# Attention with bilinear experts: three units of folded weights behind one product, the fourth ahead of the next read

## The chip, the cores and the metric

The kernel runs on one core of a Trainium2 chip. The metric is the device time of that core for one launch, in microseconds (us), lower is better. The engines are named as the profile names them: PE is TensorE, with PEld its weight loads, DVE is VectorE, ACT is ScalarE, SP is the queue that issues most DMAs.

## The reference

```python
scores = x @ state.T / sqrt(D);  a = softmax(scores);   xread = a @ state      # B=8, H=8, S=512, Ns=32, D=64
scores2 = state @ x.T / sqrt(D); a2 = softmax(scores2); sread = a2 @ x
rows = concat([xread, sread], axis=2)   # per batch 512 + 32 rows of 512
out = (((rows @ w1) * (rows @ w2)) @ w3) @ w_out                               # 512 -> 1024 -> 1024 -> 512
```

Everything is float32, and there is no nonlinearity behind the product of `rows @ w1` and `rows @ w2`.

## The kernel before

**Algebra.** `w3 @ w_out` is multiplied out once (`wo`). For the 512 x rows of a batch the read `a @ state` is not made: the state is multiplied into the weights instead. Such a product of one half of the hidden columns and of `w1` or `w2` is a **unit** (`unit` in `sw_steps`, L275 to L280): 16 matmuls by `per_head` (L148) into a two-bank PSUM tile, then `split` (L95): ACT casts it to a high part (`sw_hi`, L98) and DVE subtracts that from the tile to get the low part (`sw_lo`, L99). A batch needs four units; the first two serve its hidden tiles 0 to 3, the last two its tiles 4 to 7. Large products are made of such pairs, as high x high + high x low + low x high.

**Batches.** Batch 0 and the weights' preparation come first. Batches 1 to 7 run in `quarter_batch` (L513), one after the other, and at the end `state_rows` makes the rows of `sread`. One batch has two stages:

- Stage one is a loop over eight hidden tiles. A tile is 12 matmuls on L318 (6 for `w1`, 6 for `w2`), which fill a two-bank PSUM tile `ps`. ACT copies one bank out (`tmp`, L521), DVE multiplies it with the other (`hidden_quarters`, L401), and then the PSUM tile is free. Behind tile 1 stand three more things in PE's order: the batch's state read (L250, 64 matmuls, `reads[b]`), then the scores of the next batch (L148, 16 matmuls with `x_d`).
- Stage two (`stage2_quarters`, L453) multiplies the eight tiles by `wo` in seven products of halves: four on L432/L437, three on L444/L449. Behind the first product stand two units of the next batch, behind the second the other two.

**The softmaxes** (`scores`, L180) work on the scores of the next batch in one two-bank PSUM tile. DVE takes the maxima of the state softmax (L194), transposes the tile for the x softmax (L191) and scales the maxima (L195); ACT then makes the two exponentials of the state softmax (L204, each followed by the read of its accumulator). These are the last readers of that PSUM tile. L211 to L228 are the x softmax on DVE and ACT, whose result `at` is the moving operand of the next batch's stage one. `scores` is a generator: it goes on by one `yield` behind tile 2, one behind tile 4 and to its end behind the second product. At its end 16 DMAs move blocks of the exponentials (`e<-work`, L172), for the next state read.

**Order.** PE and SP issue in the order in which the code is written. ACT and DVE are ordered by a list scheduler when the program is built, within `high_priority` and `issue_after` constraints; on the chip each engine works its list in order.

**PSUM.** `two_banks` (L92) hands out three buffers in turn. Tiles, scores, units and the three products on L444 all take from it, so a tile waits for the release of whatever stands three requests before it. Before the change the requests behind tile 1 are: scores, tile 2, tile 3, tile 4. Tile 4 thus takes the scores' buffer.

Of the kernel before, what the change touches and what calls it, by code (L numbers as in the profile page):

```python
# [27 lines left out]
ALU = mybir.AluOpType  # L28
# [8 lines left out]
PLAIN = 1  # L37

@with_exitstack
def attn_bilinear_kernel(  # L40
# [10 lines left out]
    nc = tc.nc  # L51
# [124 lines left out]
    def attention_steps(b):  # L176
        xd = x_tiles[b]
        a2 = {}

        def scores():  # L180

            ps = two_banks()
            per_head(ps, b, lambda rows, j: xd[rows, j])
            yield
            flat = lambda t: t.rearrange("p k s -> p (k s)")

            s1 = work_tile()
            m2 = att.tile([P, KT], F32, name="m2")

            def turn():  # L190
                nc.vector.transpose(out=flat(s1), in_=flat(ps))  # L191

            def maxima():
                nc.vector.tensor_reduce(out=m2, in_=ps, axis=AX.X, op=ALU.max)  # L194
                nc.vector.tensor_scalar_mul(m2, m2, -SCALE)  # L195

            for step in (maxima, turn) if b > PLAIN else (turn, maxima):
                step()
            e2 = att.tile([P, KT, S], F32, name="e2", bufs=1)
            sum2 = att.tile([P, KT], F32, name="sum2")  # L200
            a2["e"], a2["sum"] = e2, sum2
            for kt in range(KT):
                one = slice(kt, kt + 1)
                nc.scalar.activation(  # L204
                    out=e2[:, kt], in_=ps[:, kt], func=AF.Exp, bias=m2[:, one], scale=SCALE, accum_out=sum2[:, one]
                )

            J = KT * S // NS
            s1v = flat(s1).rearrange("p (j n) -> p j n", n=NS)
            m1 = att.tile([P, J], F32, name="m1")  # L210
            nc.vector.tensor_reduce(out=m1, in_=s1v, axis=AX.X, op=ALU.max)  # L211
            nc.vector.tensor_tensor(
                out=s1v, in0=s1v, in1=m1.unsqueeze(2).broadcast_to([P, J, NS]), op=ALU.subtract
            )
            nc.scalar.activation(out=s1, in_=s1, func=AF.Exp, scale=SCALE)
            yield
            nc.vector.tensor_scalar_add(sum2, sum2, 1e-9)
            nc.vector.reciprocal(out=sum2, in_=sum2)
            sum1 = att.tile([P, J], F32, name="sum1")
            nc.vector.tensor_reduce(out=sum1, in_=s1v, axis=AX.X, op=ALU.add)  # L220
            nc.vector.tensor_scalar_add(sum1, sum1, 1e-9)
            nc.vector.reciprocal(out=sum1, in_=sum1)
            nc.vector.tensor_tensor(
                out=s1v, in0=s1v, in1=sum1.unsqueeze(2).broadcast_to([P, J, NS]), op=ALU.mult
            )
            yield
            at = work_tile()
            nc.vector.transpose(out=flat(at), in_=flat(s1))  # L228
            at_tiles[b] = [att.tile([P, KT, S], F32R, name=f"at_{part}", bufs=1) for part in ("hi", "lo")]
            last = split(*at_tiles[b], at)  # L230
            yield

            blocks = work_tile()
            with tc.issue_after(last[1].ins):
                nc.vector.transpose(out=flat(blocks), in_=flat(e2))
            a2["t"] = work_tile() if b < PLAIN else att.tile([P, KT, S], F32, name="e2", bufs=1)
            tiles = lambda t: t.rearrange("p k (t m) -> p (k t) m", m=P)
            move_blocks(lambda its, j: tiles(a2["t"])[its, :, j * NS:(j + 1) * NS],
                        lambda mine, c: tiles(blocks)[mine, :, c * NS:(c + 1) * NS])

        def read_state():

            xs = token_tiles[b]

            ps = (bank() if b else two_banks()[:, 0])[:, :KT * D].rearrange("p (k d) -> p k d", k=KT)
            for kt in range(KT):
                for t in range(NT):
                    for j in range(NP):
                        mine = slice(j * NS, (j + 1) * NS)
                        nc.tensor.matmul(  # L250
                            ps[mine, kt], a2["t"][:, kt, t * P + j * NS:t * P + (j + 1) * NS],
                            xs[:, t, 2 * j + kt], start=(t == 0), stop=(t == NT - 1),
                        )
            scaled = att.tile([P, KT, D], F32, name="scaled", bufs=1)
            a2["read"] = nc.vector.tensor_tensor(
                out=scaled, in0=ps, in1=a2["sum"].unsqueeze(2).broadcast_to([P, KT, D]), op=ALU.mult
            )
            turned = att.tile([P, KT, D], F32, name="turned")
            nc.vector.transpose(
                out=turned.rearrange("p k d -> p (k d)"), in_=scaled.rearrange("p k d -> p (k d)")  # L260
            )
            yield
            move_blocks(lambda its, j: sread[its, j, b * NS:(b + 1) * NS],
                        lambda mine, c: turned.rearrange("p k (c n) -> p (k c) n", n=NS)[mine, c])

        return scores, read_state, a2


# [3 lines left out]
    def sw_steps(b):  # L272
        sw_tiles.setdefault(b, {})

        def unit(half, i):  # L275
            ps = two_banks()
            as_q = ps.rearrange("p k (c f) -> p k c f", c=2)
            per_head(as_q, b, lambda rows, j: w_sb[rows, 2 * half:2 * half + 2, i, j])
            sw_tiles[b][half, i] = sw_pair()
            split(*sw_tiles[b][half, i], ps)  # L280

        return [(lambda half=half, i=i: unit(half, i)) for half in range(HALF) for i in range(2)]
# [66 lines left out]
    reads = {}  # L349
# [41 lines left out]
    def hidden_quarters(a, b, ft, q):  # L391

        p, kk = divmod(ft, 2)
        first, second = slice(0, HT), slice(HT, S)
        if ft == QF:
            q["late"] = late.tile([P, QF, S], F32, name="raw")
        elif ft < QF and kk == 0:
            q["raw"].append(main.tile([P, 2, NF], F32, name="g_x", bufs=2))
        whole = q["raw"][p][:, kk] if ft < QF else q["late"][:, ft - QF]
        with tc.high_priority():  # L400
            nc.vector.tensor_tensor(out=whole, in0=a, in1=b, op=ALU.mult)  # L401
        if ft == 0:
            q["a11"], q["s3"] = quarter_pairs(), quarter_pairs()
        elif ft == QF:
            q["a12"] = quarter_pairs()
        if not kk:
            return
        raw = q["raw"][p % 2]
        if ft < QF:
            split(*q["a11"][p], raw[:, :, first])  # L410
            s3 = by_two(tmp_tile())
            nc.vector.tensor_tensor(out=s3, in0=raw[:, :, first], in1=raw[:, :, second], op=ALU.subtract)
            split(*q["s3"][p], s3)
        else:
            i = p - 2
            half = q["late"][:, 2 * i:2 * i + 2]
            split(*q["a12"][i], half[:, :, first])
            nc.vector.tensor_tensor(out=raw[:, :, second], in0=raw[:, :, second], in1=half[:, :, second], op=ALU.add)
            nc.vector.tensor_tensor(out=raw[:, :, first], in0=raw[:, :, second], in1=raw[:, :, first], op=ALU.subtract)
            nc.vector.tensor_tensor(out=half[:, :, first], in0=half[:, :, first], in1=raw[:, :, first], op=ALU.subtract)  # L420
# [32 lines left out]
    def stage2_quarters(b, q, units, more):  # L453
# [56 lines left out]
        sum3(m1, bank_f)  # L510
        stored_quarter(m1, 0, 1)

    def quarter_batch(b):  # L513
        q = {"raw": []}
        w = sw_steps(b + 1) if b + 1 < B else [lambda: None] * 4
        softmax = iter(())
        for ft in range(FT):
            ps = stage1_sums(b, ft)
            a_sb = tmp_tile()
            with tc.high_priority():  # L520
                nc.scalar.copy(out=a_sb, in_=ps[:, 0])  # L521
            hidden_quarters(a_sb, ps[:, 1], ft, q)
            if ft == 1:
                run([reads[b]])
                if b + 1 < B:
                    scores, reads[b + 1], _ = attention_steps(b + 1)
                    softmax = scores()
                    next(softmax)
                    load_tokens(b + 1)
                if b + 2 < B:  # L530
                    load_x(b + 2)
            elif ft in (2, 4):
                next(softmax, None)
            if b == PLAIN and ft == 1:
                combine_weights(QF - 1)
        stage2_quarters(b, q, w[:2], [*w[2:], lambda: softmax])

    def run(steps):
        for step in steps:
# [204 lines left out]
```

## Time and profile before

| | |
|---|---|
| median of 3 runs | 491.81 us (491.71 to 491.94) |
| the profiled execution's own time | 491.68 us |
| its span | 489.9 us |
| PE busy | 483.7 us (99%), granted clock 1.0 |
| DVE busy | 390.3 us (80%) |
| ACT busy | 238.6 us (49%) |

The span is what the profile covers; the remaining 1.8 us lie around it. A busy PE is not a PE at its peak, since matmuls are pipelined and their ends are modelled: where PE waits is seen better in the start times of its instructions. Batch 1 lies at about 119.6 to 168.4 us of the span, batch 4 at 264.9 to 313.1 us, and `state_rows` begins at about 452 us.

### The profile page before, as it was taken

What the parts mean: (1) busy time and instruction counts of PE and PEld (TensorE: products, weight loads), DVE (VectorE), ACT (ScalarE), POOL (GpSimd) and SP (SyncE); (2) the same over time, 40 slices, a digit from 0 to 9 for tenths busy, and PEclk for the clock granted to TensorE, in tenths of its full rate; (3) what the DMA queues carried; (4) which work ended last, traced back from release to release, by engine and by line L of the source; (5) the groups of instructions that cost most, each with busy time, mean ns of one, the idle gap of its engine ahead of it and who ended that gap; (6) DMA issues with size and microseconds to landing.
All of it is one profiled execution on the core that took longest, in us unless ns stands there. A gap on an engine that the chain in (4) does not pass through costs nothing.

```text
span 489.9 us, 8603 instructions
## 1 busy us (share of the span) xinstructions
PE 483.7 (99%) x3390; PEld 369.0 (75%) x3390; DVE 390.3 (80%) x576; ACT 238.6 (49%) x364; POOL 0.2 (0%) x4
## 2 busy tenths in 40 slices
PE   8999999999999999999999999999999999999996
PEld 6444467767787878787888778877887788899885
DVE  5669897699899779958995899599859985578870
ACT  4767794454357045704570556055505650354640
POOL 0000000000000000000000000000000000000000
PEclk9999999999999999999999999999999999999999
DMA  8995971153113404130423042204220222001101
GB/s 341 391 405 177 371 300 27 17 216 64 36 24 160 110 25 179 35 97 4 180 45 86 5 180 50 80 5 179 48 82 6 89 52 78 7 2 43 45 2 43
DMA packets 56361, 52.49 MB, mean 107 GB/s; under 512 B 42752, under 2 KB 50944, under 8 KB 51712
## 3 DMA queue, kind: packets, MB, share of 16 engines
q1 hardware_dynamic: 47488, 43.27, 26.7%
q10 hardware_dynamic: 8832, 8.65, 5.1%
q8 instruction: 27, 0.44, 0.4%
q14 instruction: 14, 0.11, 0.1%
HBM read 38.27 MB, written 8.91 MB: 96 GB/s over the span
## 4 chain that ended last, share of the span: by engine, by line
PE 92%; DVE 3%; ACT 2%; DMA 1%; issue 0%; ACTq 0%; DVEq 0%
PE ps L318 34%; PE ps_o L432 11%; PE ps L444 8%; PE ps L148 7%; PE ps_o L332 7%; PE ps_o L437 5%; PE ps L449 4%; PE ps L682 3%; PE ps_o L575 3%; PE ps_o L562 3%; PE ps L562 3%; PE ps L684 2%; PE ps_o L250 1%; DMA raw<-in_w_k_dram 1%; DVE m L194 0%; ACT ulps L127 0%
## 5 line engine op out<-in xcount | busy, mean ns | idle before, releaser
L318 PE MATMUL ps<-at_lo,sw_hi 128*128 128x512 f32 x256 | 101.8, 398 | 0.2 <-ACT e L204 0.2
L318 PE MATMUL ps<-at_hi,sw_hi 128*128 128x512 f32 x256 | 99.8, 390 | 0.0
L318 PE MATMUL ps<-at_hi,sw_lo 128*128 128x512 f32 x256 | 99.6, 389 | 0.0
L521 ACT COPY tmp<-ps 128x512 f32<-128x512 f32 x56 | 32.8, 586 | 125.1 <-PE ps L318 114.3
L318 PEld LDWEIGHTS ps<-at_lo,sw_hi 128*128 128x128 f32 x256 | 48.1, 188 | 17.8 <-DVE g_x L401 5.4
L318 PEld LDWEIGHTS ps<-at_hi,sw_lo 128*128 128x128 f32 x256 | 48.1, 188 | 10.3
L318 PEld LDWEIGHTS ps<-at_hi,sw_hi 128*128 128x128 f32 x256 | 48.1, 188 | 9.5 <-issue 0.2
L460 DVE TENSOR_TENSOR tmp<-tmp,ps 128x512 f32<-128x512 f32 x42 | 28.9, 687 | 16.9 <-PE ps L449 15.9
L401 DVE TENSOR_TENSOR g_x<-tmp,ps 128x512 f32<-128x512 f32 x28 | 19.1, 682 | 28.7 <-ACT tmp L521 28.7
L99 DVE TENSOR_TENSOR sw_lo<-ps,sw_hi 128x1024 fp32r<-128x1024 f32 (+1 forms) x34 | 38.2, 1145 | 0.2 <-ACT sw_hi L98 0.2
L98 ACT CAST g_hi<-raw 128x512 fp32r<-128x512 f32 x42 | 24.1, 618 | 23.7 <-DVE raw L401 14.5
L98 ACT CAST sw_hi<-ps 128x1024 fp32r<-128x1024 f32 (+1 forms) x34 | 31.1, 966 | 2.8 <-PE ps L148 2.7
L432 PEld LDWEIGHTS ps_o<-wo,g_hi 128*128 128x128 f32 x224 | 28.2, 191 | 5.6 <-issue 5.0
L99 DVE TENSOR_TENSOR g_lo<-raw,g_hi 128x512 fp32r<-128x512 f32 x42 | 28.0, 681 | 5.2 <-PE ps_o L437 2.8
L432 PEld LDWEIGHTS ps_o<-t,g_hi 128*128 128x128 f32 x224 | 27.8, 192 | 5.0 <-issue 5.0
L98 ACT CAST g_hi<-g_x 128x512 fp32r<-128x512 f32 x42 | 26.0, 622 | 11.4 <-DVE g_x L401 6.0
L148 PE MATMUL ps<-w_sb,st 64*32 64x512 f32 (+1 forms) x544 | 31.4, 570 | 0.0
L432 PE MATMUL ps_o<-t,g_hi 128*128 128x256 f32 x224 | 29.8, 286 | 0.0
L432 PE MATMUL ps_o<-wo,g_hi 128*128 128x256 f32 x224 | 29.7, 286 | 0.0
L99 DVE TENSOR_TENSOR g_lo<-g_x,g_hi 128x512 fp32r<-128x512 f32 x42 | 27.4, 678 | 1.8 <-PE ps_o L437 1.8
L575 PE MATMUL ps_o<-w_sb,w 128*128 128x512 f32 x64 | 28.5, 599 | 0.0
L444 PE MATMUL ps<-t,g_hi 128*128 128x512 f32 x112 | 28.0, 392 | 0.0
(103 smaller groups left out, 785.0 us busy)
## 6 DMA issues: line engine op xcount, KB each, us to landing
raw<-in_w_k_dram SPq DMA_DIRECT2D x8, 1024.0 KB, 6.3
x_d<-in_x_d_dram SPq DMA_DIRECT2D x8, 1024.0 KB, 6.6
raw<-in_w_dram SPq DMA_DIRECT2D x8, 1024.0 KB, 6.3
x_s<-in_x_s_dram SPq DMA_DIRECT2D x8, 1024.0 KB, 5.0
out_dram<-tmp ACTq DMA_DIRECT2D x56, 128.0 KB, 1.8
raw<-in_w3t_dram SPq DMA_DIRECT2D x4, 1024.0 KB, 5.9
e<-work SPq DMA_DIRECT2D x112, 32.0 KB, 2.0
sread<-turned SPq DMA_DIRECT2D x128, 4.0 KB, 1.7
```

The costliest lines, as they stand in the source:

```text
L98: nc.scalar.copy(out=hi, in_=src),
L99: nc.vector.tensor_tensor(out=lo, in0=src, in1=hi.bitcast(F32), op=ALU.subtract),
L148: nc.tensor.matmul(ps[j * NS:(j + 1) * NS, q], sts[b][rows, j], moving(rows, j), start=True, stop=True)
L318: nc.tensor.matmul(ps[:, i], w[:, kt, c:c + P], a[:, kt], start=(k == 0), stop=(k == 3 * KT - 1))
L332: nc.tensor.matmul(ps[:, :DO], g, wo[w][:, ft, :], start=(ft == 0 and k == 0), stop=(ft == FT - 1 and k == 2))
L432: nc.tensor.matmul(ps[:, tt * HO:(tt + 1) * HO], g, w(part, k), start=(fresh and k == 0 and tt == 0 and part == "lo"), stop=False, skip_gr ...
L437: nc.tensor.matmul(ps[:, tt * HO:(tt + 1) * HO], g, w("hi", k), start=False, stop=(k == QF - 1), skip_group_check=True)
L444: nc.tensor.matmul(ps[:, tt].rearrange("p (n d) -> p n d", n=2), g, w(k), start=(k == 0), stop=False, skip_group_check=True,)
L460: sum2 = lambda out, x, y: nc.vector.tensor_tensor(out=out, in0=x, in1=y, op=ALU.add)
L521: nc.scalar.copy(out=a_sb, in_=ps[:, 0])
L562: nc.tensor.matmul(w34_ps[i][:, :DO], chunks[k][:, DO + i * P:DO + (i + 1) * P], w_out[k], start=(k == 0), stop=(k == FT - 1),)
L575: nc.tensor.matmul(w34_ps[i][:, :DO], w3s[i][:, k * P:(k + 1) * P], w_out[k], start=(k == 0), stop=(k == FT - 1))
```

## The change

Four edits, which belong together:

1. `stage2_quarters` gets three units (`units[:3]`) behind the first product of halves and none behind the second, where only the rest of the softmax stands.
2. The fourth unit is kept in `late_units` and runs in the next batch behind tile 1, ahead of the state read and of the scores. In batch 1 that list is empty.
3. For the scores made in these batches, `scores` has one more `yield`, between the exponentials of the state softmax and the x softmax.
4. Behind tile 2 the generator goes on twice; the second piece, the start of the x softmax (L211), is held back until tile 2's product on DVE (L401) has been issued.

```diff
                 nc.scalar.activation(
                     out=e2[:, kt], in_=ps[:, kt], func=AF.Exp, bias=m2[:, one], scale=SCALE, accum_out=sum2[:, one]
                 )
+            if b > PLAIN:
+                yield
...
         with tc.high_priority():
-            nc.vector.tensor_tensor(out=whole, in0=a, in1=b, op=ALU.mult)
+            q["whole"] = nc.vector.tensor_tensor(out=whole, in0=a, in1=b, op=ALU.mult)
...
+    late_units = []
+
     def quarter_batch(b):
         q = {"raw": []}
-        w = sw_steps(b + 1) if b + 1 < B else [lambda: None] * 4
...
             if ft == 1:
-                run([reads[b]])
+                run([*late_units, reads[b]])
...
-            elif ft in (2, 4):
+            elif ft == 2:
+                next(softmax, None)
+                with tc.issue_after(q["whole"].ins):
+                    next(softmax, None)
+            elif ft == 4:
                 next(softmax, None)
...
-        stage2_quarters(b, q, w[:2], [*w[2:], lambda: softmax])
+        units = sw_steps(b + 1) if b + 1 < B else []
+        late_units[:] = units[3:]
+        stage2_quarters(b, q, units[:3], [lambda: softmax])
```

How the instructions stand now is shown at three places of batch 4. Lines of the changed kernel are two or three higher from L211 on (L211 became L213, L401 L403, L432 L434, L521 L524); a number behind a name tells one buffer from another.

PE, behind the first product of halves (`wo,g_hi` and `wo,g_lo`); `w_sb,st` is a unit, `t` stands for the combined weights of the second product. Before:

```order
L437 MATMUL ps_o<-wo,g_lo 128x256 x8
L148 MATMUL ps_2852<-w_sb,st 32x512 x8
L148 MATMUL ps_2865<-w_sb,st 32x512 x8
L432 MATMUL ps_o<-t,g_hi 128x256 x16
L437 MATMUL ps_o<-t,g_lo 128x256 x8
L148 MATMUL ps_2912<-w_sb,st 32x512 x8
L148 MATMUL ps_2925<-w_sb,st 32x512 x8
L432 MATMUL ps_o<-wo,g_hi 128x256 x16
```

Now, the same place:

```order
L439 MATMUL ps_o<-wo,g_lo 128x256 x8
L148 MATMUL ps_2852<-w_sb,st 32x512 x8
L148 MATMUL ps_2865<-w_sb,st 32x512 x8
L148 MATMUL ps_2878<-w_sb,st 32x512 x8
L434 MATMUL ps_o<-t,g_hi 128x256 x16
L439 MATMUL ps_o<-t,g_lo 128x256 x8
L434 MATMUL ps_o<-wo,g_hi 128x256 x16
```

The third product now follows the second directly. The unit that is missing here stands in the next batch between the last matmul of tile 1 and the state read.

DVE, from tile 1's product to tile 2's (`g_x<-tmp,ps_2684`); `g_lo` are low parts of tiles 0 and 1, `scaled` and `turned` belong to the state read, `m_2702` are the maxima of the state softmax and `ps_2669` the scores. Before:

```order
L401 TENSOR_TENSOR g_x<-tmp,ps_2594 128x512
L412 TENSOR_TENSOR tmp<-g_x 128x512
L255 TENSOR_TENSOR scaled<-ps_o,sum_2173 128x128
L99 TENSOR_TENSOR g_lo<-g_x,g_hi 128x512
L99 TENSOR_TENSOR g_lo<-tmp,g_hi 128x512
L259 STREAM_TRANSPOSE turned<-scaled 128x128
L194 TENSOR_REDUCE m_2702<-ps_2669 128x2
L191 STREAM_TRANSPOSE work<-ps_2669 128x1024
L195 TENSOR_SCALAR m_2702<-m_2702 128x2
L211 TENSOR_REDUCE m_2710<-work 128x32
L401 TENSOR_TENSOR g_x<-tmp,ps_2684 128x512
```

Now:

```order
L403 TENSOR_TENSOR g_x<-tmp,ps_2581 128x512
L414 TENSOR_TENSOR tmp<-g_x 128x512
L99 TENSOR_TENSOR g_lo<-g_x,g_hi 128x512
L99 TENSOR_TENSOR sw_lo<-ps_2603,sw_hi 128x1024
L99 TENSOR_TENSOR g_lo<-tmp,g_hi 128x512
L257 TENSOR_TENSOR scaled<-ps_o,sum_2173 128x128
L261 STREAM_TRANSPOSE turned<-scaled 128x128
L194 TENSOR_REDUCE m_2702<-ps_2669 128x2
L191 STREAM_TRANSPOSE work<-ps_2669 128x1024
L195 TENSOR_SCALAR m_2702<-m_2702 128x2
L403 TENSOR_TENSOR g_x<-tmp,ps_2684 128x512
L213 TENSOR_REDUCE m_2710<-work 128x32
```

The low part of the fourth unit (`sw_lo`) now stands ahead of the scores' maxima, and the x softmax begins behind tile 2's product instead of ahead of it.

ACT, from the copy of tile 1 to the exponentials (`e_2706`) and the copies of tile 2 (`ps_2684`) and tile 3 (`ps_2714`). Before:

```order
L521 COPY tmp<-ps_2594 128x512
L98 CAST g_hi<-g_x 128x512
L98 CAST g_hi<-tmp 128x512
L521 COPY tmp<-ps_2684 128x512
L204 ACTIVATE e_2706,sum_2707<-ps_2669,m_2702 128x512 x2
L521 COPY tmp<-ps_2714 128x512
```

Now:

```order
L524 COPY tmp<-ps_2581 128x512
L98 CAST g_hi<-g_x 128x512
L98 CAST sw_hi<-ps_2603 128x1024
L98 CAST g_hi<-tmp 128x512
L204 ACTIVATE e_2706,sum_2707<-ps_2669,m_2702 128x512
L524 COPY tmp<-ps_2684 128x512
L204 ACTIVATE e_2706,sum_2707<-ps_2669,m_2702 128x512
L524 COPY tmp<-ps_2714 128x512
```

The unit's cast is new here, and the copy of tile 2 moved from ahead of both exponentials to between them. Batches 2, 3, 5 and 6 read the same at these two places. In batch 1, which has no late unit, this stretch of both engines is as before; batch 7 has the late unit and no scores.

## Prediction

> **What bounds the kernel now.** I read the page first, then the chain of work that ended last, then the timeline of each engine in one batch.
>
> ```profile
> PE 483.7 (99%) x3390; PEld 369.0 (75%) x3390; DVE 390.3 (80%) x576; ACT 238.6 (49%) x364; POOL 0.2 (0%) x4
> ```
>
> The chain in the window of batch 4 (start, length, what) consists of PE alone:
>
> ```profile
> 265.05 5.46 PE ps L318 x24
> 270.52 1.03 PE ps_o L250 x64
> 271.55 1.02 PE ps L148 x16
> 272.57 16.66 PE ps L318 x72
> ...
> 292.10 1.88 PE ps L148 x32
> 293.98 2.11 PE ps_o L432 x16
> ...
> 298.92 2.11 PE ps_o L432 x16
> ...
> 302.00 1.92 PE ps_o L432 x16
> ...
> 313.26 0.93 PE ps L318 x4
> ```
>
> A batch takes 313.26 - 265.05 = 48.21 us, and PE works through it without a visible hole. So an edit counts only if it shortens PE's own list or makes PE wait. Waits of 0.1 us show in the start times. Here PE goes from tile 3 to tile 4 of batch 4, and then PEld at the same place:
>
> ```profile
> 277.84 0.39 PE L318 MATMUL ps<-at_hi,sw_lo 128*128 128x512 f32 x1
> 278.07 0.49 PE L318 MATMUL ps<-at_lo,sw_hi 128*128 128x512 f32 x1
> 278.39 0.40 PE L318 MATMUL ps<-at_hi,sw_hi 128*128 128x512 f32 x1
> ...
> 278.05 0.19 PEld L318 LDWEIGHTS ps<-at_lo,sw_hi 128*128 128x128 f32 x1 [0.25 <-ACT e L204]
> ```
>
> Tile 4's first weights waited 0.25 us for the exponentials, which read the scores out of the buffer that tile 4 takes. PE lost 0.1 us by it (0.32 us from start to start, where its neighbour has 0.23). This handover is already just in time: whatever comes later there, PE waits for in full.
>
> **The change part by part.** The frame is batch 4; batches 2 to 6 have the same new order.
>
> *Fewer turns on PE.* The product on L432 takes 2.11 us behind units and 1.92 us behind another product, 0.19 us less. Before, two products of a batch stand behind units, now one. The units themselves stay four a batch, at 1.88 / 2 = 0.94 us each. No row shows a unit between tile 1 and the state read: the nearest is the x16 group of the scores, 1.02 us, against 0.94 in a pair. So the move costs between 0 and 0.08 us; it could be below nothing only if the read behind it got shorter, for which I see no reason. I take 0, since the place already changes from L318 to small matmuls once. Six batches (1 to 6) save 6 x 0.19 = 1.14 us.
>
> *The late unit on DVE and ACT.* Here are the two engines' lists as they ran before; for the unit's price, a pair of casts and one subtraction with its follower.
>
> ```profile
> 270.55 0.59 ACT L521 COPY tmp<-ps 128x512 f32<-128x512 f32 x1 [2.13 <-PE ps L318]
> 271.89 0.62 ACT L98 CAST g_hi<-g_x 128x512 fp32r<-128x512 f32 x1 [0.75 <-DVE g_x L401]
> 272.62 0.62 ACT L98 CAST g_hi<-tmp 128x512 fp32r<-128x512 f32 x1
> 275.60 0.59 ACT L521 COPY tmp<-ps 128x512 f32<-128x512 f32 x1 [2.36 <-PE ps L318]
> 276.56 0.69 ACT L204 ACTIVATE e<-ps,m 128x512 f32<-128x512 f32 x1 [0.36 <-DMA sread<-turned]
> ...
> 277.24 0.68 ACT L204 ACTIVATE e<-ps,m 128x512 f32<-128x512 f32 x1
> 277.81 0.19 ACT L204 ACTIVATION_READ_ACCUMULATOR e<-ps,m 128x1 f32 x1
> 278.27 0.59 ACT L521 COPY tmp<-ps 128x512 f32<-128x512 f32 x1 [0.26 <-PE ps L318]
> ...
> 293.36 1.93 ACT L98 CAST sw_hi<-ps 128x1024 fp32r<-128x1024 f32 x2
> ```
>
> ```profile
> 271.17 0.69 DVE L401 TENSOR_TENSOR g_x<-tmp,ps 128x512 f32<-128x512 f32 x1 [2.03 <-ACT tmp L521]
> 271.89 0.69 DVE L412 TENSOR_TENSOR tmp<-g_x 128x512 f32<-128x512 f32 x1
> 272.50 0.28 DVE L255 TENSOR_TENSOR scaled<-ps_o,sum 128x128 f32<-128x128 f32 x1
> 272.70 0.68 DVE L99 TENSOR_TENSOR g_lo<-g_x,g_hi 128x512 fp32r<-128x512 f32 x1
> 273.30 0.68 DVE L99 TENSOR_TENSOR g_lo<-tmp,g_hi 128x512 fp32r<-128x512 f32 x1
> 273.91 0.30 DVE L259 STREAM_TRANSPOSE turned<-scaled 128x128 f32<-128x128 f32 x1
> 274.13 1.18 DVE L194 TENSOR_REDUCE m<-ps 128x2 f32<-128x1024 f32 x1
> 275.24 1.23 DVE L191 STREAM_TRANSPOSE work<-ps 128x1024 f32<-128x1024 f32 x1
> 276.39 0.12 DVE L195 TENSOR_SCALAR m<-m 128x2 f32<-128x2 f32 x1
> ...
> 295.95 1.22 DVE L99 TENSOR_TENSOR sw_lo<-ps,sw_hi 128x1024 fp32r<-128x1024 f32 x1
> 297.09 1.23 DVE L235 STREAM_TRANSPOSE work<-e 128x1024 f32<-128x1024 f32 x1
> ```
>
> DVE waited 2.03 us ahead of 271.17, so it has no earlier backlog, and up to there the change moves nothing. From start to start the rows give what each step holds DVE: 0.60 for a half-size subtraction, 0.20 for L255, 0.22 for L259, 1.11 for L194, 1.15 for L191, 1.14 for the unit's low part.
>
> Now the new order. ACT: g_hi at 271.89; the unit's cast follows at about 272.45 (the unit itself is off PE by about 271.5) and takes a little over 1.93 / 2, to 273.45. DVE: L412 at 271.89, g_lo at 272.55, the unit's low part at 273.45 to 274.6, the other g_lo to 275.2, L255 (L259 waits for its end, 0.28) to 275.5, L259 to 275.7, the maxima to 276.8, the transpose to 278.0, L195 done at 278.1. Before, that was 276.51: 1.6 us earlier, of which 1.14 are the low part and the rest the wait for its cast and for L255.
>
> ACT then: first exponential at 278.15; 0.68 later (276.56 to 277.24), at 278.83, the copy of tile 2, which was ready by 276.6 and stood in the list behind that exponential; the second exponential at about 279.35; its accumulator is read 0.76 later (277.24 to 278.00), at 280.1. PE goes on at 280.1.
>
> Without that wait tile 4 would begin at 278.07 + 0.94 = 279.0, since the late unit stands ahead of it. So PE now waits 280.1 - 279.0 = 1.1 us in each of batches 2 to 6, five times: 5 x 1.1 = 5.5 us. The 0.1 us that PE lost before by restarting is lost as before. Bounds: without the copy in between, the wait is 0.55; with every copy and cast at its full length and 0.08 for the unit's new place, 1.25. I take 1.1, which is nearest to the rows.
>
> The unit's own buffer is free in time: its low part ends at 274.65, and tile 3, which takes it, begins at about 276.2.
>
> *The x softmax behind tile 2's product.* DVE now waits for the copy of tile 2 from 278.1 to about 279.45, with L211 behind it in its list; before, L211 filled that time. L211 thus moves from 276.5 to about 280.05, 3.5 us, of which PE's own shift is 0.94 + 1.1 = 2.0: DVE runs 1.5 us late against the tiles. This costs nothing, because of two covers. Stage two: before, DVE caught up there and waited for the next product:
>
> ```profile
> 304.57 1.29 DVE L99 TENSOR_TENSOR g_lo<-raw,g_hi 128x512 fp32r<-128x512 f32 x2 [0.48 <-ACT g_hi L98]
> 307.71 1.41 DVE L460 TENSOR_TENSOR tmp<-tmp,ps 128x512 f32<-128x512 f32 x2 [1.85 <-PE ps L449]
> ```
>
> That is 0.48 + 1.85 = 2.3 us of room, and another 1.14 since one low part less is made there. Transposed blocks: L235 now stands behind two low parts and comes about 3.6 us later (2.0 by PE's shift, the rest DVE's lag); its 16 DMAs on SP's queue and the read that needs them were
>
> ```profile
> 298.38 11.49 SPq L172 DMA_DIRECT2D e<-work  x16
> ...
> 318.72 1.03 PE ps_o L250 x64
> ```
>
> so issued by 309.87, with 8.8 us to the read, which itself moves 0.94 us back. If this cover were gone, each us late would cost a us in each of five batches.
>
> *The three units in a row* need the buffers of tiles 5, 6 and 7; the third begins at least 1.92 + 1.88 = 3.8 us behind tile 7's last matmul, and that tile's copy and product (0.59 + 0.69) end, 1.5 us late, after 2.8. Free.
>
> **The sum.** 5.5 - 1.14 = +4.4 us on the profiled execution's own 491.68 us (span 489.9): 496.0 us. That execution stands 0.13 us below the median of the runs, which is less than the rounding of the wait.
>
> **A rule against it.** Batch 1 already has a longer wait of this kind; its row of the windows (length, busy times, granted clock, DMA) and the matmul behind that wait:
>
> ```profile
> 119.64:168.40 48.76, 48.56 (x385) 38.81 (x384) 44.44 (x68) 23.58 (x38) 0.00 (x0) 1.00 0.26 76
> ...
> 136.15 0.50 PE L318 MATMUL ps<-at_lo,sw_hi 128*128 128x512 f32 x1 [0.20 <-ACT e L204]
> ```
>
> The granted clock stayed at 1.00, and I leave PE's rate as it is. The Trainium skill, "TensorE: Matmul & The Clock Gate", section "A second HAM failure mode: psum-queue depth-cycling", tells of a kernel whose PE idled briefly between groups while it went round its PSUM buffers, and whose clock then swung to half. The trace does not show that for a wait of this length; no run here has five of 1.1 us. It is the third rival below.
>
> **The rivals.**
>
> 1. *The exponentials are still in time* (faster). Only the merged units count: 491.68 - 1.14 = 490.5. For it: tile 4 begins 0.94 us later, which gives the exponentials that much more time. Against: DVE's and ACT's lists are fixed, and the unit's low part alone takes 1.14 us ahead of the maxima. It decides at the maxima: L195 would have to be done by about 277.0 instead of 278.1.
> 2. *A part of the wait only.* If the copy of tile 2 costs the second exponential little, or the two small waits on DVE don't arise, the wait is 0.2 to 0.6 us: -0.1 to +1.9, thus 491.6 to 493.5.
> 3. *The clock drops behind each wait* (slower still). One tile at half rate costs its own length again, 16.66 / 6 = 2.78 us, five times 13.9: about 510.
> 4. *DVE does not catch up.* If half a microsecond a batch of its lag reached PE in stage two: 5 x 0.5 = +2.5, 498.5.
>
> That the change does nothing is out: PE's, DVE's and ACT's lists do differ.
>
> **How the numbers follow.** About 0.2% (1 us) is what a measurement of this kernel can tell from no change. Forecast 80%; rival 1, 6%; rival 2, 8%, half of it within 1 us of before; rival 3, 2%; rival 4, 4%. So faster 6%, same 4%, slower 90%. Within the forecast the bounds are 5 x 0.9 - 1.14 = +3.4 and 5 x 1.25 - 6 x 0.1 = +5.7 (units that merge at half the gain), 495.1 to 497.4. The range takes in the upper part of rival 2's side and the first steps of rival 4: 494.4 to 497.8.
>
> **What would show it.** Right: in the changed profile, batches 2 to 6 take 48.21 + 1.1 - 0.19 = 49.1 us each; PEld's wait for the exponentials ahead of tile 4 is the longest wait on PE and 1.1 to 1.3 us; L195 ends about 7.6 us behind tile 1's last matmul (270.5), where it was 6.0; the copy of tile 2 begins behind the first exponential; the third product of halves takes 1.92 us; the granted clock is 1.00. Wrong: tile 4 starting with no gap, or a new wait of PE in stage two or ahead of the state read.

## The result, and the profile after

The changed kernel takes 497.05 us (median, 496.77 to 497.30), before beside it 491.88: a ratio of 1.0102, interval 1.0085 to 1.0120. Its profiled execution took 496.86 us, with a span of 495.1, so +5.2 us in the span.

The page's line of engines has the same PE work as before, in a longer span:

```profile
PE 483.6 (98%) x3390; PEld 368.8 (74%) x3390; DVE 389.6 (79%) x576; ACT 236.0 (48%) x364; POOL 0.2 (0%) x4
```

The chain in batch 4 of the changed kernel (start, length, what). Before, tiles 2 to 7 stood in it as one piece of 16.66 us. Now it leaves PE behind tile 2 (the x12 piece), runs through ScalarE's exponentials and the copy of tile 2, and comes back to PE at tile 4; tile 3 is not in it:

```profile
266.37 5.47 PE ps L320 x24
271.83 1.02 PE ps L148 x16
...
274.90 2.97 PE ps L320 x12
277.87 1.67 issue
279.54 0.07 ACT e L204
...
280.12 0.19 ACT e L204
280.32 0.47 ACT tmp L524
280.79 0.69 ACT e L204 x2
...
281.52 11.18 PE ps L320 x48
...
295.57 2.73 PE ps L148 x48
298.30 2.11 PE ps_o L434 x16
...
301.37 1.92 PE ps_o L434 x16
...
315.51 0.69 PE ps L320 x3
```

The same place in PE's timeline (start, length, engine, line, operation; in brackets the idle time before it and what ended it). Tile 4's first matmul starts 1.34 us behind the last of tile 3 (neighbours stand 0.23 apart), and the profile names the releaser:

```profile
280.18 0.39 PE L320 MATMUL ps<-at_hi,sw_lo 128*128 128x512 f32 x1
281.52 0.50 PE L320 MATMUL ps<-at_lo,sw_hi 128*128 128x512 f32 x1 [0.95 <-ACT e L204]
281.86 0.40 PE L320 MATMUL ps<-at_hi,sw_hi 128*128 128x512 f32 x1
```

ScalarE and VectorE ahead of it. The copy of tile 2 (L524) stands between the exponentials, and L195 ends 279.45 - 271.83 = 7.6 us behind tile 1's last matmul. The profile names no releaser for the first exponential ("issue"); it starts 0.09 us behind the end of L195, whose maxima it needs:

```profile
279.54 0.69 ACT L204 ACTIVATE e<-ps,m 128x512 f32<-128x512 f32 x1 [4.28 <-issue]
...
280.22 0.57 ACT L524 COPY tmp<-ps 128x512 f32<-128x512 f32 x1
280.68 0.70 ACT L204 ACTIVATE e<-ps,m 128x512 f32<-128x512 f32 x1
```

```profile
274.78 1.22 DVE L99 TENSOR_TENSOR sw_lo<-ps,sw_hi 128x1024 fp32r<-128x1024 f32 x1 [0.22 <-ACT sw_hi L98]
...
277.07 1.19 DVE L194 TENSOR_REDUCE m<-ps 128x2 f32<-128x1024 f32 x1
278.18 1.23 DVE L191 STREAM_TRANSPOSE work<-ps 128x1024 f32<-128x1024 f32 x1
279.33 0.12 DVE L195 TENSOR_SCALAR m<-m 128x2 f32<-128x2 f32 x1
280.82 0.69 DVE L403 TENSOR_TENSOR g_x<-tmp,ps 128x512 f32<-128x512 f32 x1 [1.37 <-ACT tmp L524]
```

PE's waits by what ended them (total, times, longest). The five waits of the first row are those at tile 4 of batches 2 to 6. The second row is one that the prediction did not have; it lies in stage two of batch 1:

```profile
PE ps L320 <- ACT e L204: 4.8, 5, 1.0
...
PE ps_o L434 <- ACT tmp L482: 0.3, 1, 0.3
```

Batch 4's row of the windows gives its length and the granted clock, 1.00:

```profile
266.37:315.51 49.14, 48.19 (x385) 38.91 (x385) 40.02 (x58) 21.13 (x35) 0.00 (x0) 1.00 0.26 79
```

**Where the 5.2 us are.** Batches 2 to 6 are 49.14 us long instead of 48.21: 5 x 0.93 = 4.7. The rest, 0.5, is the new wait of batch 1 (about 0.45, experiment 7) and small change; the late units only moved work from batches 1 to 6 into 2 to 7.

### The profile page after: what moved, and what is told of

It reads as the page before. It is cut to its first block, busy times and chain, and to the rows that moved or that the text cites. A ratio compares the mean times of both kernels' runs of the same rounds, so it can differ in the third digit from the quotient of the medians.

```text
span 495.1 us, 8617 instructions
## 1 busy us (share of the span) xinstructions
PE 483.6 (98%) x3390; PEld 368.8 (74%) x3390; DVE 389.6 (79%) x576; ACT 236.0 (48%) x364; POOL 0.2 (0%) x4
## 4 chain that ended last, share of the span: by engine, by line
PE 88%; ACT 4%; DVE 3%; issue 3%; DMA 1%; ACTq 0%; DVEq 0%
PE ps L320 32%; PE ps_o L434 11%; PE ps L446 8%; PE ps L148 7%; PE ps_o L334 7%; PE ps_o L439 5%; PE ps L451 4%; PE ps L691 3%; PE ps_o L584 3%; PE ps_o L571 3%; PE ps L571 3%; PE ps L693 2%; PE ps_o L252 1%; ACT e L204 1%; DMA raw<-in_w_k_dram 1%
## 5 line engine op out<-in xcount | busy, mean ns | idle before, releaser
L524 ACT COPY tmp<-ps 128x512 f32<-128x512 f32 x56 | 32.8, 585 | 112.9 <-PE ps L320 101.5
L403 DVE TENSOR_TENSOR g_x<-tmp,ps 128x512 f32<-128x512 f32 x28 | 19.2, 686 | 34.6 <-ACT tmp L524 34.6
L434 PEld LDWEIGHTS ps_o<-t,g_hi 128*128 128x128 f32 x224 | 27.7, 191 | 5.5 <-issue 5.0
L434 PE MATMUL ps_o<-t,g_hi 128*128 128x256 f32 x224 | 29.8, 286 | 0.3 <-ACT tmp L482 0.3
L434 PE MATMUL ps_o<-wo,g_hi 128*128 128x256 f32 x224 | 29.1, 283 | 0.0
L434 PEld LDWEIGHTS ps_o<-wo,g_hi 128*128 128x128 f32 x224 | 28.3, 192 | 0.5
```

Of the source, the lines that this page charges most:

```text
L434: nc.tensor.matmul(ps[:, tt * HO:(tt + 1) * HO], g, w(part, k), start=(fresh and k == 0 and tt == 0 and part == "lo"), stop=False, skip_gr ...
```

## The experiments

**Theory A** is the prediction's: PE waits at tile 4 because the late unit's low part delays the maxima on VectorE, and the copy of tile 2 comes between the exponentials. **Theory B**: the split softmax (edits 3 and 4) causes the loss. **Theory C**: PE loses by one more turn to small matmuls, or by a lower clock behind the waits. Experiments 1 to 4 separate the parts. From experiment 5 on theory A has the buffer added, which experiment 3 brought in, and each text names its own rivals.

**Experiment 1: only the units move.** The softmax goes on as before:

```diff
-            if b > PLAIN:
-                yield
...
-            elif ft == 2:
-                next(softmax, None)
-                with tc.issue_after(q["whole"].ins):
-                    next(softmax, None)
-            elif ft == 4:
+            elif ft in (2, 4):
```

> Edits 1 and 2 alone: the fourth unit stands ahead of the next batch's read, and the softmax has the pieces it had before (the x softmax is not held back). Theory A (PE waits at tile 4 for the exponentials, which come late because the unit's cast and low part stand ahead of the maxima and a copy stands between the two exponentials): the wait stays at 1.1 us in five batches, about 497.0, like the changed kernel. Theory B (the loss comes from holding the x softmax back, which leaves DVE idle): the loss is gone, 490.7 to 491.5. Theory C (PE loses by one more turn to small matmuls ahead of the read, or by a lower clock behind the waits): about 497.0 as well.

Measured: 497.16 us, ratio 1.0106 (1.0092 to 1.0119). The units alone bring the whole loss; theory B falls. Theory C gives the same time, so this time does not decide between A and C. The waits speak for A: five of the six in this row are those at tile 4 (the sixth, 0.2 us in batch 1, is there before the change too), and the granted clock is 1.00.

```profile
PE ps L318 <- ACT e L204: 5.0, 6, 1.0
```

**Experiment 2: only the softmax is split.** Units as before:

```diff
-                run([*late_units, reads[b]])
+                run([reads[b]])
...
-        late_units[:] = units[3:]
-        stage2_quarters(b, q, units[:3], [lambda: softmax])
+        stage2_quarters(b, q, units[:2], [*units[2:], lambda: softmax])
```

> Edits 3 and 4 alone: all four units stand in stage two as before, two and two, and only the x softmax is held back behind tile 2's product. A: nothing stands ahead of the maxima, tile 4 starts as before, 491.9 within 0.4. B: the loss is here, 496 or more. C: 491.9.

Measured: 491.23 us, ratio 0.9988 (0.9979 to 0.9997), slightly better than before and 0.3 us below the range that I gave, with no wait at tile 4. A batch takes 48.09 us, 0.12 less: the restart of 0.1 us at tile 4 that the prediction had read in before is gone. Why came out of the next run.

**Experiment 3: the exponentials behind the copy.** The changed kernel, with both exponentials held behind the copy of tile 2:

```diff
-                nc.scalar.copy(out=a_sb, in_=ps[:, 0])
+                copied = nc.scalar.copy(out=a_sb, in_=ps[:, 0])
...
             elif ft == 2:
-                next(softmax, None)
+                with tc.issue_after(copied.ins):
+                    next(softmax, None)
```

> The changed kernel with one thing undone: the exponentials are issued behind the copy of tile 2, so both run back to back. A: the second exponential ends 0.5 us earlier, and PE's wait shrinks from 1.1 to about 0.55 us in five batches: 497.05 - 2.7 = 494.3. B and C: DVE's hold and PE's order are the changed kernel's, 497.0.

Measured: 490.69 us, ratio 0.9975 (0.9966 to 0.9984). This was a miss of 3.6 us: the kernel is faster than before. Its ScalarE in batch 4, then VectorE and PE at tile 4:

```profile
275.85 0.59 ACT L524 COPY tmp<-ps 128x512 f32<-128x512 f32 x1 [2.69 <-PE ps L320]
277.39 0.69 ACT L204 ACTIVATE e<-ps,m 128x512 f32<-128x512 f32 x1 [0.96 <-DMA sread<-turned]
...
278.07 0.68 ACT L204 ACTIVATE e<-ps,m 128x512 f32<-128x512 f32 x1
```

```profile
277.23 0.13 DVE L195 TENSOR_SCALAR m<-m 128x2 f32<-128x2 f32 x1
277.27 0.68 DVE L403 TENSOR_TENSOR g_x<-tmp,ps 128x512 f32<-128x512 f32 x1
```

```profile
278.08 0.39 PE L320 MATMUL ps<-at_hi,sw_lo 128*128 128x512 f32 x1
278.31 0.39 PE L320 MATMUL ps<-at_lo,sw_hi 128*128 128x512 f32 x1
278.54 0.39 PE L320 MATMUL ps<-at_hi,sw_hi 128*128 128x512 f32 x1
```

Tile 4 starts at 278.31 while the second exponential still reads the scores, until 278.75. So tile 4 does not take the scores' buffer here. The semaphores in the traces say the same. In before, in the changed kernel and in experiment 1, the first weight load of tile 4 in batches 2 to 6 waits for ScalarE's semaphore, thus for the exponentials: tile 4 has the scores' buffer. In experiments 2, 3 and 4 it waits for VectorE's, thus for the product of tile 2: it has the buffer that tile 2 leaves, and tile 5, 2.7 us later, waits for ScalarE's and has the scores'. My expectation had kept the buffer of the changed kernel.

**Experiment 4: the late unit behind tile 0.** The rest as changed:

```diff
-            if ft == 1:
-                run([*late_units, reads[b]])
+            if ft == 0:
+                run(late_units)
+            elif ft == 1:
+                run([reads[b]])
```

> The changed kernel with the late unit one place earlier, behind tile 0 instead of tile 1; its low part then falls into a 2 us hole of DVE, ahead of tile 1's product. A: tile 4 no longer waits for more than before (0 to 0.1 us); what is left are the merged units (6 x -0.19), the new turns (6 x 0.08 into the unit, 6 x 0.1 back into a tile) and batch 1's wait in stage two (0.45): 492.3, between 491.7 and 492.8. B: the x softmax is held back as in the changed kernel, 497. C: one turn more than the changed kernel, 497 to 498.

Measured: 492.30 us, ratio 1.0006 (0.9997 to 1.0015): the wait at tile 4 is gone with the low part's place, and theory C, which gave 497 to 498, falls. It too has the other buffer, and the copy of tile 2 stands ahead of the exponentials again, so the time alone does not tell these apart. Batch 4's rows (ScalarE, then PE at tile 4) help:

```profile
276.06 0.59 ACT L524 COPY tmp<-ps 128x512 f32<-128x512 f32 x1 [2.36 <-PE ps L320]
...
277.69 0.68 ACT L204 ACTIVATE e<-ps,m 128x512 f32<-128x512 f32 x1
...
278.52 0.39 PE L320 MATMUL ps<-at_lo,sw_hi 128*128 128x512 f32 x1
```

The second exponential ends 0.15 us ahead of tile 4, as it does in before (277.92 and 278.07). So with the scores' buffer tile 4 would have lost about the 0.1 us that it loses in before, and no more; that build was not run.

**Experiments 5 and 6: the buffer by itself.** The buffers are now handed out by a list, with each engine's instructions in the same order as in the kernel that they start from. 5 is the changed kernel with experiment 3's buffers; 6 is experiment 3 with the changed kernel's buffers, that is without the numbers from 43 on:

```diff
+    turns, asked = [0, 1, 2], []
+    SWAPPED = (16, 27, 43, 59, 75, 91, 107)
...
     def two_banks():
-        return ps_2.tile([P, 2, NF], F32, name="ps_2")
+        n = turns.pop(1 if len(asked) in SWAPPED else 0)
+        turns.append(n)
+        asked.append(n)
+        return ps_2.tile([P, 2, NF], F32, name=f"ps_2_{n}", bufs=1)
```

> The changed kernel with every engine's instructions in the same order, but in batches 2 to 6 tile 4 writes into the PSUM buffer that tile 2 has left, and tile 5 into the scores' buffer, where the changed kernel has them the other way round. Theory A (the order on ScalarE and the buffer both have to be changed, since with the copy of tile 2 between the exponentials either buffer comes free late): in the changed kernel's batch 4 the second exponential started at 280.68 and ran 0.70, and tile 2's product, which would be waited for then, started at 280.82 and ran 0.69, so the wait at tile 4 stays, 1.1 to 1.3 us in each of the five batches, now for the product of L403: 497.1 to 497.8, say 497.5. Rival B (the buffer alone made the loss, whatever the order on ScalarE): no wait at tile 4, 491.0 to 491.8.

> The kernel with the exponentials behind the copy of tile 2, every engine's instructions in the same order as there, but tile 4 of batches 2 to 6 writes into the scores' buffer, as in the changed kernel. Theory A (order and buffer both count): with the copy first the second exponential of batch 4 ends at 278.75 to 278.84, and tile 4 started at 278.31, so tile 4 waits 0.45 to 0.65 us in five batches: 490.7 + 2.3 to 3.3 = 493.0 to 494.0, say 493.5, with PE's wait for L204 at 2.3 to 3.3 us in all. Rival B (the buffer alone counts): the whole loss is back, 496 to 497. Rival C (the order on ScalarE alone counts): 490.7, no wait.

Measured: experiment 5, 497.49 us, ratio 1.0109 (1.0091 to 1.0126); experiment 6, 494.34 us, ratio 1.0047 (1.0033 to 1.0062). PE's waits in experiment 5 (its line numbers stand 6 higher): as many, about as long, but for the product of tile 2:

```profile
PE ps L326 <- DVE g_x L409: 5.0, 5, 1.0
```

Experiment 6 at tile 4 of batch 4, ScalarE and PE:

```profile
279.97 0.68 ACT L210 ACTIVATE e<-ps,m 128x512 f32<-128x512 f32 x1
```

```profile
279.98 0.39 PE L326 MATMUL ps<-at_hi,sw_lo 128*128 128x512 f32 x1
280.79 0.50 PE L326 MATMUL ps<-at_lo,sw_hi 128*128 128x512 f32 x1 [0.43 <-ACT e L210]
281.13 0.39 PE L326 MATMUL ps<-at_hi,sw_hi 128*128 128x512 f32 x1
```

Together with the changed kernel and experiment 3 this is a complete table (us):

| | tile 4 in the scores' buffer | in tile 2's buffer |
|---|---|---|
| copy between the exponentials | 497.05 | 497.49 |
| copy ahead of the exponentials | 494.34 | 490.69 |

The buffer alone gains nothing (+0.4), the order alone 2.7, both 6.4. With the copy in between, both buffers come free late, at 281.38 and 281.51 in the changed kernel. With the copy first, tile 2's is free at 277.95, ahead of tile 4's turn, and the scores' is 0.4 late. In experiment 6 a wait listed as 0.43 costs more: 0.81 - 0.23 = 0.58 from start to start, and another 0.1 to the second matmul (0.34 instead of 0.23); a batch is 0.73 longer than in experiment 3. I had left out both extras, so the 494.34 lies 0.3 above the range that I gave for it.

**Experiment 7: batch 1 as before.** Experiment 3, with batch 1's four units in their old places. In the changed kernel's batch 1, ScalarE has the cast of `at_hi` ahead of the copy of L482, and PE's fourth product waits for that copy:

```profile
154.95 1.05 ACT L98 CAST at_hi<-work 128x1024 fp32r<-128x1024 f32 x1 [1.82 <-DVE work L230]
155.90 0.58 ACT L482 COPY tmp<-ps_o 128x512 f32<-128x512 f32 x1
```

```profile
155.14 1.12 PE L439 MATMUL ps_o<-wo,g_lo 128*128 128x256 f32 x8
156.53 2.18 PE L434 MATMUL ps_o<-t,g_hi 128*128 128x256 f32 x16 [0.27 <-ACT tmp L482]
```

What the wait costs follows from the batch: without a wait batch 1 would have become shorter by the unit that it hands on and by the merge, 0.94 + 0.19 = 1.13 us; it went from 48.83 to 48.15, 0.68. The wait costs the difference, 0.45.

```diff
-        late_units[:] = units[3:]
-        stage2_quarters(b, q, units[:3], [lambda: softmax])
+        first = 2 if b == PLAIN else 3
+        last = units[first:] if b == PLAIN else []
+        late_units[:] = units[3:] if b > PLAIN else []
+        stage2_quarters(b, q, units[:first], [*last, lambda: softmax])
```

> The kernel with the exponentials behind the copy of tile 2, but batch 1 computes all its four units of w as before the change (two behind the first product, two behind the second), so that batch 2 has no late unit. Theory A (the changed batch 1 lost 0.45 us in a wait of stage two for the copy of L482, which stands behind a cast of the softmax there): that wait goes, -0.45; the merge in batch 1 is lost, +0.19; the late unit that goes from batch 2 to batch 1 costs 0.94 in place of 1.02, -0.08: 490.7 - 0.35 = 490.35, with no wait of PE for L482. Rival (the wait is covered by something later in the product): 490.7 to 490.9, as little slower as the lost merge.

Measured: 490.36 us, ratio 0.9971 (0.9961 to 0.9982), with no wait for L482. It is the fastest kernel of this study, though its interval overlaps that of experiment 3. The two profiles are clearer than the medians: batches 1 and 2, the only ones that differ, take 95.71 us together instead of 96.08, 0.37 less where 0.35 was expected.

**Experiment 8: before, with the other buffer.** The kernel before, and the list of experiment 5:

> The kernel before the change, every engine's instructions in the same order, but tile 4 of batches 2 to 6 writes into the buffer that tile 2 has left and tile 5 into the scores' buffer. It asks what made the kernel with the split softmax alone 0.7 us faster than before, as its tile 4 also writes there. Theory A (in before, tile 4 waits a little for the second exponential, a gap of 0.23 us on PE in batch 4; with the other buffer it would wait for tile 2's product instead, whose copy runs at 278.27 behind the exponentials, so about 0.7 to 1.0 us later): slower, 5 x 0.7 to 5 x 1.5, 495 to 499. Rival (the buffer is what made that kernel faster): 491.2.

Measured: 493.46 us, ratio 1.0033 (1.0022 to 1.0044). Slower, as theory A says, but less than I gave: I took the copy at 278.27 for tile 2's, and it is tile 3's. Tile 2's is the one at 275.60. VectorE and PE in batch 4 of this run:

```profile
277.32 1.22 DVE L217 TENSOR_REDUCE m<-work 128x32 f32<-128x1024 f32 x1
278.45 0.68 DVE L407 TENSOR_TENSOR g_x<-tmp,ps 128x512 f32<-128x512 f32 x1
```

```profile
278.65 0.39 PE L324 MATMUL ps<-at_hi,sw_lo 128*128 128x512 f32 x1
279.19 0.50 PE L324 MATMUL ps<-at_lo,sw_hi 128*128 128x512 f32 x1
```

The product ends at 279.13, behind the x softmax's maxima, and tile 4 starts 0.31 us late: 5 x 0.31 = 1.6 us, the measured difference. So in before the scores' buffer was the better one. The split softmax puts tile 2's product ahead of those maxima, and only then is tile 2's buffer the better one; that is where experiment 2's 0.6 us (5 x 0.12) come from. Experiment 2 with the scores' buffer was not run. That it would have kept the 0.1 us of before is read from its trace, where the second exponential ends at 278.08 and tile 4 starts at 278.24, as close as in before.

**Experiment 9: the low part twice.** Experiment 3, and the late unit's subtraction made a second time:

```diff
             split(*sw_tiles[b][half, i], ps)
+            if b > PLAIN and (half, i) == (1, 1):
+                hi, lo = sw_tiles[b][half, i]
+                nc.vector.tensor_tensor(out=lo, in0=ps, in1=hi.bitcast(F32), op=ALU.subtract)
```

> The kernel with the exponentials behind the copy of tile 2 (490.69 us; tile 4 takes tile 2's buffer, which that tile's product on L403 frees), with the late unit's low part computed twice on DVE, 1.14 us more from start to start ahead of the maxima in batches 2 to 6; the result is unchanged. Theory A (what stands ahead of the maxima on DVE delays the release of either buffer, here by way of L195 and the product behind it): the product of tile 2 started at 277.27 and ran 0.68, so it ended 0.36 ahead of tile 4's start at 278.31; 1.14 later it ends at 279.09, tile 4 starts some 0.05 behind that, 0.85 us late, and 0.1 is lost in restarting: 5 x 0.95 = 4.7, 495.4 us, with a wait of PE for L403 in five batches. Rival (the place of the low part on DVE is not what counts, only the unit's on PE and the order on ScalarE): 490.7 to 491.2, no wait at tile 4.

Measured: 495.38 us, ratio 1.0057 (1.0043 to 1.0070). The total is as expected, its parts are not, and part of the agreement is chance: the kernel before took 492.48 us beside this run and 491.97 beside experiment 3, so against before the second subtraction costs 4.2 us and not the 4.7 expected. PE has two holes in batch 4, at tile 3 and at tile 4:

```profile
277.51 0.39 PE L323 MATMUL ps<-at_hi,sw_lo 128*128 128x512 f32 x1
277.93 0.47 PE L323 MATMUL ps<-at_lo,sw_hi 128*128 128x512 f32 x1
278.24 0.40 PE L323 MATMUL ps<-at_hi,sw_hi 128*128 128x512 f32 x1
...
280.53 0.39 PE L323 MATMUL ps<-at_hi,sw_lo 128*128 128x512 f32 x1
281.16 0.50 PE L323 MATMUL ps<-at_lo,sw_hi 128*128 128x512 f32 x1 [0.24 <-DVE g_x L406]
281.50 0.40 PE L323 MATMUL ps<-at_hi,sw_hi 128*128 128x512 f32 x1
```

Tile 4 loses 0.40 and 0.11 in restarting, tile 3 0.19 and 0.08, since it takes the late unit's own buffer, which the second subtraction frees later: it runs until 277.79, and it is VectorE's semaphore that tile 3's first weight load waits for. That is 0.78 a batch in place of my 0.95; batch 4 measures 0.87 more than in experiment 3 (48.77 against 47.90), the rest in steps too small to name. Work on VectorE ahead of the maxima reaches PE, by two buffers.

## Why the prediction was right

- **The late unit on VectorE and ScalarE.** This was the step that carried the sign, and it held in its parts. The changed batch 4 begins 1.32 us later than the frame (266.37 against 265.05); with that added, the prediction has L195 done at 279.42 (measured 279.45), the copy at 280.15 (280.22), the second exponential at 280.67 (280.68), PE going on at 281.42 (281.52). Its wait of 1.1 us is 1.34 - 0.23 = 1.11. Experiment 1 shows that the units alone bring it.
- **Fewer turns on PE.** Held: the third product takes 1.92 us in place of 2.11.
- **The unit's place.** I took 0, and the sum agrees, but not for the reason that I gave: alone the unit takes 1.02 us, not 0.94, and the three in a row take 2.73 instead of 3 x 0.94 = 2.82. The two cancel.
- **The x softmax behind tile 2's product.** Taken at nothing, for batches 2 to 6 rightly: VectorE still catches up in stage two and waits there,

```profile
309.96 1.41 DVE L462 TENSOR_TENSOR tmp<-tmp,ps 128x512 f32<-128x512 f32 x2 [1.91 <-PE ps L451]
```

  and PE waits for nothing there.
- **Batch 1 was missed.** I costed it by batch 4 and listed a new wait in stage two as a sign against me. There is one, in batch 1 alone: ScalarE's list puts a cast of the softmax ahead of a copy that PE needs, 0.45 us. This is over half of the difference between the +4.4 forecast and the +5.2 measured in the span; experiment 7 takes it away. By the start times of the batches the rest is 0.2 in batches 2 to 6 (49.15 - 48.21 = 0.94 a batch where the forecast has 1.1 - 0.19 = 0.91), 0.1 for the late unit in batch 7, which takes 1.02 and not the 0.94 that batch 1 saved, and 0.1 ahead of batch 1.
- **The other sign against it.** A new wait ahead of the state read is listed too, `PE ps_o L252 <- DMA e<-work: 0.2, 1, 0.2`, in batch 1 at 125.74. Experiment 8, which has the units and the softmax of before, has the same wait at 125.80, so the change does not cause it.
- **The bound on the wait.** "Without the copy in between, the wait is 0.55" holds only with the scores' buffer kept: experiment 6 has 0.58. In a build with the copy first the buffer changes too, and the wait is 0.
- **The rule on the clock.** The Trainium skill, "TensorE: Matmul & The Clock Gate", section "A second HAM failure mode: psum-queue depth-cycling", tells of a kernel in which frequent short idles of PE between its groups made the clock swing. Five waits of 1.1 us left the granted clock of each of batches 2 to 6 at 1.00, so that does not happen here for one such wait in 49 us.
- **Rivals.** None of the first three is seen: tile 4 does wait, in full, at full clock. Rival 4's sign, a new wait in stage two, is seen in batch 1 alone, and comes there from ScalarE's list.

## What to carry to other kernels

When a step moves into a stage whose engine is always busy, ask which buffer the next group takes and list everything that stands ahead of that buffer's last reader on the other engines; here one subtraction and one copy made a saving of 1.1 us into a loss of 5. Cost the first and the last round of a loop by themselves, since their lists can differ. If a group can take one of two buffers, both dates must be known, for a cure on one of them alone may gain nothing.

## What was not expected of the hardware and the program

- The buffers are not handed out strictly in turn, as the description of the kernel ahead of the prediction has it. It holds for tile 4 in batches 2 to 6 of before and of the changed kernel, but the code does not fix it: where the order on ScalarE and VectorE differed (experiments 2 to 4), so did the assignment. An edit that seems to move one instruction also moved a buffer, and that made 3.65 us (experiment 6 against 3).
- A short wait costs PE more than is listed for it: 0.43 us in the timeline was 0.58 from start to start, and the first interval after it was 0.34 us instead of 0.23.
- The 16 small matmuls of a unit cost 1.02 us alone, 1.88 in a pair of units and 2.73 for three in a row.
